# Stores of the first two batches' rows issued by SyncE in place of GpSimd, in a kernel of memory attention and two matrix products, with its written order searched anew

## Chip, cores and metric

The kernel runs on one core of one Trainium2 chip. The metric is the device time of one execution in microseconds; before the change the median of three runs is 727.82 us (727.61 to 728.73).

## The reference

All data is float32. For each of 8 batches and 8 heads, with 576 rows of 64 elements and 32 memory slots:

```python
a = softmax(phi, axis=rows)                # phi: 8 x 8 x 576 x 32
k_m = einsum('bhsm,bhsd->bhmd', a, k)      # 32 x 64 for each head
v_m = einsum('bhsm,bhsd->bhmd', a, v)
scores = q @ k_m.T / 8
attn_out = softmax(scores) @ v_m           # 8 x 8 x 576 x 64
x = attn_out.transpose(0, 2, 1, 3).reshape(4608, 512)
r = maximum(x @ w_in, 0)                   # w_in: 512 x 2048
out = (r * r) @ w_out                      # w_out: 2048 x 512, out: 4608 x 512
```

## The kernel before

**Work for one batch.** `memory(b)` loads phi, k and v and forms the sums over rows by TensorE (`products`, L545). k and v come in two parts of the rows, five chunks and then four, through one buffer, the tile KV: the first part KV_0 is two loads of 640 KB (128 partitions x 4 x 320), the second part KV_5 two loads of 512 KB (128 x 4 x 256), and both are issued by SyncE (SP) at L495. Since there is one buffer, KV_5 of a batch can be loaded only when the products on KV_0 have run. `scores(b)` loads q in four pieces (q_0_0, q_0_1, q_1_0, q_1_1), each by four DMAs on SP (L816); a piece waits until VectorE (DVE) has transposed the piece before it (L819). Then, for 16 slices of 128 of the 2048 columns, `mm1` computes x @ w_in in three terms and two halves of 288 rows (L894, six matmuls for each half), ScalarE (ACT) and DVE square the positive part, and `mm2` adds the slice to four accumulators of 128 rows each (for each accumulator L929 and L930 with the high piece of the squares, then L932 with the low piece). The 64 rows of a batch that are left over are done for two batches together (`mm2_left`, L955).

**Order of batches.** The first four slices of batch 0 run first, then all of batch 1, then the rest of batch 0, then batches 2 to 7. The sums of the first four slices of batch 0 wait in two tiles, `part`, until the rest is added to them. While batches 0 and 1 run, the weights are loaded and decoded (tiles raw and work); q, k, v and phi of batch 2 are loaded while the rest of batch 0 runs.

**Stores.** `evac` copies a finished accumulator to SBUF and records a store (L989). For batches 0 and 1 a store covers all 128 rows of an accumulator, as two rows of every partition group (`2x64x512`, 256 KB): four such stores from the tiles o_0 and o_1 of batch 1 and four from the `part` tiles of batch 0; the left-over rows of both batches (tile ol) are two stores of 128 KB. From batch 2 on a store is 64 KB (`32x512`). GpSimd (POOL) issues all of them, but for the last batch, whose stores alternate between SP and ACT.

**What sets the order.** Every instruction group is recorded by `Plan.op` with its engine or two engines that it may run on, its cost and its tiles. `Plan.order` walks through the table PLACES, 3526 numbers that name the recorded groups in the order in which they are written out (a negative one means the second of two engines). So the table fixes the order on each engine's queue; what one queue waits for from another is set by the tiles. The costs in `Plan.order` replay the table and decide one thing only: before a TensorE group that is expected to find TensorE idle, `fill` (L427) adds matmuls on zeros. There are 72 of these, all within the first 46 us of the span.

Of the kernel before, what the change touches and what calls it, by code (L numbers as in the profile page):

```python
# [341 lines left out]
def tile_attention_moe(  # L342
# [21 lines left out]
    B, H, S, D = q.shape  # L364
    M = phi.shape[3]
    DM, FF = w_in.shape
# [603 lines left out]
    def evac(a, home, o, cols, add=False):  # L970
        final = cols[-1] == (B - 1, NC - 1)
        if final:
            home = home[0]
# [5 lines left out]
        n = 1 if final or cols[0][0] >= 2 else len(cols) // len({x[0] for x in cols})  # L979
# [115 lines left out]
```

## Time and profile before

| | |
|---|---|
| median of 3 runs | 727.82 us (727.61 to 728.73) |
| profiled execution, its own time | 726.3 us |
| its span in the trace | 724.5 us |
| TensorE busy with matmuls | 711.0 us (98% of the span) |
| VectorE busy | 457.6 us (63%) |
| ScalarE busy | 344.6 us (48%) |
| GpSimd busy | 52.7 us (7%) |
| mean granted TensorE clock | 0.996 of full speed |

The span runs from the first to the last recorded instruction of the profiled execution; its own time is 1.8 us longer, for what lies around it. Of the span TensorE is idle for 13.5 us in all, so the table alone says that the other engines matter where they make TensorE wait, and a look by stretches of the span has to tell where that is.

### The profile page before, as it was taken

What the parts mean: (1) busy time and instruction counts of PE and PEld (TensorE: products, weight loads), DVE (VectorE), ACT (ScalarE), POOL (GpSimd) and SP (SyncE); (2) the same over time, 40 slices, a digit from 0 to 9 for tenths busy, and PEclk for the clock granted to TensorE, in tenths of its full rate; (3) what the DMA queues carried; (4) which work ended last, traced back from release to release, by engine and by line L of the source; (5) the groups of instructions that cost most, each with busy time, mean ns of one, the idle gap of its engine ahead of it and who ended that gap; (6) DMA issues with size and microseconds to landing.
All of it is one profiled execution on the core that took longest, in us unless ns stands there. A gap on an engine that the chain in (4) does not pass through costs nothing.

```text
span 724.5 us, 13808 instructions
## 1 busy us (share of the span) xinstructions
PE 711.0 (98%) x5487; PEld 574.2 (79%) x5490; DVE 457.6 (63%) x1082; ACT 344.6 (48%) x788; POOL 52.7 (7%) x108
## 2 busy tenths in 40 slices
PE   8899999989999999999999999999999999999997
PEld 4478888877788888888887887888878887888886
DVE  5999999823874579545873347745587355854430
ACT  3589998744442343533542434552343333534330
POOL 0000000010001000210001100050002100060000
PEclk9999999999999999999999999999999999999999
DMA  9933643555036131342203211242311301030002
GB/s 336 345 128 96 197 148 117 162 148 162 1 98 173 32 97 33 101 145 62 62 1 98 86 42 57 61 133 70 99 32 30 115 1 32 1 91 1 1 1 72
DMA packets 40608, 66.46 MB, mean 92 GB/s; under 512 B 8224, under 2 KB 24608, under 8 KB 40544
## 3 DMA queue, kind: packets, MB, share of 16 engines
q1 hardware_dynamic: 32928, 56.77, 25.6%
q0 software_dynamic: 7136, 8.16, 4.2%
q8 instruction: 43, 0.70, 0.4%
q10 hardware_dynamic: 480, 0.66, 0.3%
q14 instruction: 21, 0.17, 0.1%
HBM read 56.10 MB, written 9.44 MB: 90 GB/s over the span
## 4 chain that ended last, share of the span: by engine, by line
PE 89%; DMA 5%; DVE 4%; ACT 1%; issue 0%; SPq 0%; DVEq 0%; ACTq 0%
PE h L894 26%; PE acc L929 16%; PE acc L932 16%; PE acc L930 15%; PE accl L955 6%; PE vwpv L786 4%; DMA raw<-in_moe_w_in_dram 2%; DMA KV<-in_v_dram 2%; PE pkv_pa L545 1%; PE pscpa L826 1%; PE pkv_pv L545 1%; DMA KV<-in_k_dram 1%; DMA raw<-in_moe_w_out_dram 0%; DVE work L463 0%; PE idle L427 0%
## 5 line engine op out<-in xcount | busy, mean ns | idle before, releaser
L894 PE MATMUL h<-ath,vw 128*128 128x288 f32 x1024 | 210.6, 296 | 0.1
L929 PE MATMUL acc<-wo,gh 128*128 128x512 f32 x512 | 204.0, 398 | 0.0
L930 PE MATMUL acc<-wo,gh 128*128 128x512 f32 x512 | 201.5, 394 | 0.0
L894 PEld LDWEIGHTS h<-ath,vw 128*128 128x128 f32 x1024 | 170.4, 188 | 20.3 <-ACT r L898 3.3
L932 PE MATMUL acc<-wo,glo 128*128 128x512 f32 x512 | 181.8, 397 | 0.0
L898 ACT ACTIVATE r<-h 128x288 f32<-128x288 f32 x173 | 68.4, 408 | 151.7 <-PE h L894 124.9
L932 PEld LDWEIGHTS acc<-wo,glo 128*128 128x128 f32 x512 | 94.7, 188 | 28.6 <-issue 8.8
L929 PEld LDWEIGHTS acc<-wo,gh 128*128 128x128 f32 x512 | 96.2, 188 | 25.7 <-issue 9.1
L900 ACT ACTIVATE gh<-r 128x512 fp32r<-128x512 f32 x128 | 80.6, 629 | 75.2 <-PE acc L930 58.3
L904 DVE TENSOR_TENSOR glo<-r,gh 128x512 fp32r<-128x512 f32 x128 | 87.5, 683 | 45.4 <-ACT r L902 19.8
L930 PEld LDWEIGHTS acc<-wo,gh 128*128 128x128 f32 x512 | 96.3, 188 | 17.1
L894 PE MATMUL h<-atl,vw 128*128 128x288 f32 x512 | 109.5, 295 | 0.0
L894 PEld LDWEIGHTS h<-atl,vw 128*128 128x128 f32 x512 | 82.1, 188 | 0.0
L989 POOL DMA_DIRECT2D out_dram<-o x84 | 42.7, 514 | 486.9 <-ACT o L398 401.5
L899 DVE TENSOR_SCALAR r<-h 128x288 f32<-128x288 f32 x83 | 37.0, 454 | 61.6 <-PE h L894 60.5
L902 ACT ACTIVATE r<-r 128x576 f32<-128x576 f32 x100 | 68.2, 683 | 2.1
L955 PE MATMUL accl<-wo,gl 128*128 128x512 f32 x192 | 48.3, 395 | 0.0
L905 DVE TENSOR_TENSOR gl<-r,gl 128x64 fp32r<-128x64 f32 x128 | 27.4, 217 | 26.1 <-ACT r L902 25.6
L955 PEld LDWEIGHTS accl<-wo,gl 128*128 128x128 f32 x192 | 35.4, 188 | 8.4 <-issue 1.0
L901 ACT ACTIVATE gl<-r 128x64 fp32r<-128x64 f32 x128 | 31.4, 251 | 19.4 <-DVE r L899 18.5
L903 DVE TENSOR_TENSOR r<-r 128x576 f32<-128x576 f32 x28 | 21.1, 754 | 20.1 <-ACT gl L901 13.4
L398 ACT CAST vw<-vwpv 128x256 fp32r<-128x256 f32 x48 | 16.8, 376 | 24.8 <-PE vwpa L786 18.3
(140 smaller groups left out, 707.6 us busy)
## 6 DMA issues: line engine op xcount, KB each, us to landing
q<-in_q_dram SPq DMA_DIRECT2D x96, 136.0 KB, 2.8
raw<-in_moe_w_in_dram SPq DMA_DIRECT2D x16, 512.0 KB, 4.9
raw<-in_moe_w_out_dram SPq DMA_DIRECT2D x16, 512.0 KB, 4.3
out_dram<-o POOLq DMA_DIRECT2D x80, 64.0 KB, 2.1
phi<-in_phi_dram SPq DMA_DIRECT2D x8, 576.0 KB, 5.2
KV<-in_v_dram SPq DMA_DIRECT2D x6, 640.0 KB, 4.4
KV<-in_k_dram SPq DMA_DIRECT2D x6, 640.0 KB, 6.0
KV<-in_k_dram SPq DMA_DIRECT2D x6, 512.0 KB, 6.0
```

The lines of the kernel that those rows point to most:

```text
L894: nc.tensor.matmul(p()[:, 0:n], V()[:, l, hh, c0:c0 + P], x()[:, hh, cs], start=(i == 0), stop=(i == 5))
L898: op({"ACT": 295, **({} if b < 2 else {"DVE": tt(n)})}, lambda e, cs=cs, n=n, p=p: nc.scalar.activation(r()[:, cs], p()[:, 0:n], AF.Relu) ...
L899: else nc.vector.tensor_scalar(r()[:, cs], p()[:, 0:n], 0.0, None, ALU.max), [p], [(r, h)])
L900: op({"ACT": 535}, lambda e: nc.scalar.activation(gh(), r()[:, 0:SM], AF.Square), [r], [gh])
L901: op({"ACT": 160}, lambda e: nc.scalar.activation(G()[:, 0, lc], r()[:, SM:S], AF.Square), [r], [(G, (b % 2, 0))])
L902: op({"ACT": act(S), **({} if b < 2 else {"DVE": tt(S)})}, lambda e: nc.scalar.activation(r(), r(), AF.Square) if e == "ACT" else nc.vecto ...
L904: vec({"DVE": tt(SM)}, lambda e: nc.vector.tensor_sub(glo(), r()[:, 0:SM], gh().bitcast(F32)), [r, gh], [glo])
L929: nc.tensor.matmul(a(), gh()[:, c], t()[:, 0], start=f0, stop=False)
L930: nc.tensor.matmul(a(), gh()[:, c], t()[:, 1], start=False, stop=False)
L932: nc.tensor.matmul(a(), glo()[:, c], t()[:, 0], start=False, stop=f1)
L955: nc.tensor.matmul(a(), G()[:, l, :], t()[:, w], start=(ff == 0 and n == 0), stop=(ff == NFF - 1 and n == 2))
L989: d(rows, o()[32 * j:32 * (j + n), :])
```

## The change

One line of `evac` gives the stores of more than 64 KB to SP where POOL issued them, and the size that the planner's replay reckons with for any such store is raised (a factor of 75 in place of 48). The table PLACES is replaced by another.

```diff
 PLACES = (
...
-            dma(store, 48 * n * DM * 4, [home], [], eng=("SP", "ACT")[j // n % 2] if final or b == B - 1 else "POOL")
+            dma(store, 75 * n * DM * 4, [home], [], eng=("SP", "ACT")[j // n % 2] if final or b == B - 1 else "SP" if n > 1 else "POOL")
```

`n` is 4 for the accumulators of batches 0 and 1 and 2 for their left-over rows, so ten stores move from POOL to SP: four of o_0 and o_1, four of the part tiles, two of ol. The stores of batches 2 to 6 stay on POOL. The counts of TensorE's groups are the same (1536 matmuls of L894, 512 each of L929, L930 and L932, 192 of L955); of the fill matmuls there are 71 in place of 72.

SP's queue around the loads of k and v of batch 2 (KV_1826 and KV_1978 before, KV_1825 and KV_1980 after the change) stood like this before:

```order
L495 DMA KV_0_1826<-in_v_dram 128x4x320
L495 DMA KV_0_1826<-in_k_dram 128x4x320
L816 DMA q_0_0_1865<-in_q_dram 32x2x544 x4
L495 DMA KV_5_1978<-in_k_dram 128x4x256
L495 DMA KV_5_1978<-in_v_dram 128x4x256
L816 DMA q_0_1_2000<-in_q_dram 32x2x544 x4
L816 DMA q_1_0_2074<-in_q_dram 32x2x544 x4
L495 DMA phi_2126<-in_phi_dram 128x4x288
```

and stands like this now:

```order
L495 DMA KV_0_1825<-in_k_dram 128x4x320
L495 DMA KV_0_1825<-in_v_dram 128x4x320
L816 DMA q_0_0_1865<-in_q_dram 32x2x544 x4
L495 DMA KV_5_1980<-in_v_dram 128x4x256
L495 DMA KV_5_1980<-in_k_dram 128x4x256
L816 DMA q_0_1_2007<-in_q_dram 32x2x544 x4
L989 DMA out_dram<-o_0_1993 2x64x512
L816 DMA q_1_0_2110<-in_q_dram 32x2x544 x4
L989 DMA out_dram<-o_1_1926 2x64x512
```

The first two stores of batch 1 now stand behind both KV_5 loads and behind q_0_1, one ahead of q_1_0 and one behind it; phi of the next batch follows later.

On POOL the stores had stood one behind the other, with nothing but the accumulators to wait for:

```order
L989 DMA out_dram<-o_0_1898 2x64x512
L989 DMA out_dram<-o_1_1910 2x64x512
L989 DMA out_dram<-part_983 2x64x512
L989 DMA out_dram<-part_1010 2x64x512
L989 DMA out_dram<-ol_2847 64x512 x2
```

and its queue has now, behind the last instruction of the preparation, the 64-KB stores of batch 2 alone:

```order
L613 MEMSET kb_0_382 128x256
L989 DMA out_dram<-o_0_3642 32x512
L989 DMA out_dram<-o_1_3660 32x512 x3
```

Later on SP's queue, around KV_5 of batch 3 (KV_2699) and KV_0 of batch 4 (KV_2809), the rest of the moved stores stands now between loads:

```order
L989 DMA out_dram<-o_1_1926 2x64x512
L816 DMA q_0_1_2425<-in_q_dram 32x2x544 x4
L495 DMA KV_5_2699<-in_k_dram 128x4x256
L495 DMA KV_5_2699<-in_v_dram 128x4x256
L816 DMA q_1_0_2717<-in_q_dram 32x2x544 x4
L989 DMA out_dram<-part_999 2x64x512 x2
L989 DMA out_dram<-part_1009 2x64x512
L495 DMA KV_0_2809<-in_k_dram 128x4x320
L495 DMA KV_0_2809<-in_v_dram 128x4x320
L989 DMA out_dram<-part_1009 2x64x512
L989 DMA out_dram<-o_0_1993 2x64x512
L495 DMA phi_2888<-in_phi_dram 128x4x288
```

The last store of o_1 stands ahead of these two KV_5 loads with a q piece between; behind them four stores of part and the last of o_0 stand ahead of the next phi.

On TensorE the second products of batch 2 (L545 on KV_5) stood before the change behind this work on the rest of batch 0:

```order
L929 MATMUL acc_4_0_2030<-wo_1099,gh_2040 128x512
L930 MATMUL acc_4_0_2030<-wo_1099,gh_2040 128x512
L932 MATMUL acc_4_0_2030<-wo_1099,glo_2057 128x512
L545 MATMUL pkv_pa<-KV_5_1978,phi_1018 32x128
```

and now behind this:

```order
L929 MATMUL acc_4_0_2026<-wo_1136,gh_1983 128x512
L930 MATMUL acc_4_0_2026<-wo_1136,gh_1983 128x512
L932 MATMUL acc_4_2_2013<-wo_1136,glo_2005 128x512
L545 MATMUL pkv_pa<-KV_5_1980,phi_731 32x128
```

Between the first products (on KV_0) and the second (on KV_5) there were 5 halves of L894 with six matmuls each, 10 pairs of L929 and L930, and 8 matmuls of L932; now there are 4, 9 and 6. The order of the other groups changes all through the program, by a few places for the most part.

## Rows read from the trace of the kernel before

**Rows 1.** Page, part 1: busy time of TensorE, share of the span, instructions.

```profile
PE 711.0 (98%) x5487; PEld 574.2 (79%) x5490; DVE 457.6 (63%) x1082; ACT 344.6 (48%) x788; POOL 52.7 (7%) x108
```

**Rows 2.** Windows of TensorE: stretch, length, busy (count), granted clock, DMA share, GB/s.

```profile
0.00:50.00 50.00, 42.94 (x609) 1.00 0.76 276
50.00:160.00 110.00, 107.60 (x793) 1.00 0.49 151
160.00:700.00 540.00, 540.00 (x4015) 1.00 0.23 64
```

**Rows 3.** Waits of TensorE, its longest: us in total, times, longest.

```profile
PE pkv_pa L545 <- DMA KV<-in_v_dram: 2.3, 1, 2.3
PE pvt L591 <- DVE kx L676: 1.5, 2, 1.0
```

**Rows 4.** Timeline of TensorE around that wait: start, duration, in brackets idle time before.

```profile
156.22 0.39 PE L932 MATMUL acc<-wo,glo 128*128 128x512 f32 x1
158.92 0.27 PE L545 MATMUL pkv_pa<-KV,phi 64*32 64x128 f32 x1 [2.31 <-DMA KV<-in_v_dram]
```

**Rows 5.** Timeline of SP, its DMA issues from 146 us: start, time to issue.

```profile
146.05 0.38 SPq L495 DMA_DIRECT2D KV<-in_k_dram  x1
146.47 1.34 SPq L495 DMA_DIRECT2D KV<-in_v_dram  x1
147.99 15.92 SPq L816 DMA_DIRECT2D q<-in_q_dram  x8
```

**Rows 6.** Tile KV, window 145:148 (KV_5 of batch 2): issue to landing.

```profile
DMA to landing us min/median/max: 11.2/11.7/12.3
```

**Rows 7.** Windows over the second products, all engines: the clock is third from last.

```profile
159.00:160.00 1.00, 1.00 (x52) 1.00 (x59) 0.00 (x0) 0.00 (x0) 0.00 (x0) 0.61 0.37 111
160.00:161.00 1.00, 1.00 (x31) 0.62 (x14) 0.00 (x0) 0.00 (x0) 0.00 (x0) 0.50 0.08 23
161.00:162.00 1.00, 1.00 (x4) 0.89 (x5) 0.62 (x1) 0.00 (x0) 0.00 (x0) 0.50 0.06 17
162.00:163.00 1.00, 1.00 (x4) 0.41 (x3) 0.78 (x5) 0.37 (x1) 0.00 (x0) 0.69 0.00 0
```

**Rows 8.** Timeline of POOL, 138 to 170 us: the four stores of batch 1.

```profile
142.97 0.95 POOL L989 DMA_DIRECT2D out_dram<-o  x1 [116.82 <-ACT o L398]
144.83 0.82 POOL L989 DMA_DIRECT2D out_dram<-o  x1 [0.92 <-ACT o L398]
150.16 1.59 POOL L989 DMA_DIRECT2D out_dram<-o  x2 [4.51 <-ACT gl L901]
```

**Rows 9.** Tile KV, window 134:137 (KV_0 of batch 2).

```profile
DMA to landing us min/median/max: 4.3/5.3/6.2
```

**Rows 10.** Tile KV, window 383:386 (KV_5 of batch 5).

```profile
DMA to landing us min/median/max: 4.1/5.5/6.8
```

**Rows 11.** Tile KV, window 473:475 (KV_5 of batch 6, among 64-KB stores).

```profile
DMA to landing us min/median/max: 5.5/6.5/7.5
```

**Rows 12.** Tile KV, window 312:314 (beside one big store of part).

```profile
DMA to landing us min/median/max: 7.2/9.9/12.6
```

**Rows 13.** Windows with two big stores in flight alone (224:226), and one (the others).

```profile
224.00:226.00 2.00, 2.00 (x43) 1.51 (x44) 0.00 (x0) 0.41 (x1) 0.00 (x0) 1.00 0.25 102
321.00:323.00 2.00, 2.00 (x35) 0.90 (x36) 0.51 (x2) 1.18 (x4) 0.00 (x0) 1.00 0.13 51
```

**Rows 14.** Chain that ended last, 143 to 166 us: start, time to the next, group.

```profile
142.96 0.23 PE acc L932
143.19 0.24 PE acc L929
143.90 0.80 PE h L894 x6
```

**Rows 15.** Window of all engines in the preparation; DVE is the third busy time.

```profile
30.00:40.00 10.00, 8.54 (x63) 4.56 (x64) 10.00 (x21) 6.12 (x13) 0.00 (x0) 1.00 0.69 270
```

**Rows 16.** Page, part 6: loads of q, size of one, median from issue to landing.

```profile
q<-in_q_dram SPq DMA_DIRECT2D x96, 136.0 KB, 2.8
```

270 rows, old and new, of the table PLACES are left out of this document.

## Prediction

> **What bounds the kernel now.** I read the page first: TensorE is busy with matmuls for 711.0 of 724.5 us [rows 1], so no other engine is the bound, and what a new order can win is the 13.5 us in which TensorE stands idle, and time in which its clock is low. The windows say where the idle time lies: 7.06 us in the first 50 us, 2.4 us from 50 to 160, none from 160 to 700 [rows 2]; the rest is the start of the tail. The waits name what ended each: the largest single one, and the only one over 0.3 us behind the first 50 us, is 2.3 us of the products of L545 for a load of KV [rows 3]. The timeline puts it at 156.22 to 158.92, ahead of the second products of batch 2 [rows 4]. The next view is SP's queue: that load, KV_5, was issued at 146.05 and 146.47 [rows 5] and took 11.2 and 12.3 us to land [rows 6], so the later one was there at 158.8.
>
> The stall costs more than itself. In the windows behind it the granted clock is 0.61, 0.50, 0.50 and 0.69 in the four microseconds from 159 to 163, and TensorE is busy for all of them [rows 7]: it has gone from the upper of its two levels, 2.4 GHz, to 1.2 GHz, after 2.3 us of standing idle. Work done at those shares leaves (1 - 0.61) + 0.50 + 0.50 + (1 - 0.69) = 1.70 us to be made up. Stall and clock together are 2.31 + 1.70 = 4.0 us.
>
> **Why the load is late.** Four stores of 256 KB are issued by POOL at 142.97, 144.83, 150.16 and just behind it [rows 8], two before the loads and two while they are in flight. In other places the same kind of load takes far less: 6.2 us for the later of the pair at 135 [rows 9], 6.8 at 384 [rows 10], 7.5 at 474 amid 64-KB stores [rows 11]; but 12.6 us at 312, beside one big store [rows 12]. How such a store can hold up a load of only twice its size shows where it is alone in flight: the DMA engines are 0.13 busy, which is 2 of 16, and move 51 GB/s [rows 13], so 262,144 bytes keep two engines for about 5.1 us, and a load that is spread over all sixteen ends with the part that these two carry. With two such stores in flight the share is 0.25 at 102 GB/s, so POOL's two stores lay on different pairs.
>
> **Part by part.** *The stall.* On SP's queue no big store now stands ahead of KV_5 since the preparation; the first stands behind both loads and a q piece, and SP gives out its transfers in order. So I take KV_5 at the price of the quiet rows: the later load lands 6.2 us after its own issue, the issue is 0.42 us behind the first [rows 5, 9], so 6.6 us after the first issue; bounds 6.6 and 7.9 (7.5 + 0.4, [rows 11]). The cover shrinks also. Before, TensorE worked from the first issue, 146.05, to 156.22 + 0.23 = 156.45, that is 10.4 us. The new order takes out one half of L894 (0.80), one pair (0.24 + 0.23, L930 taken like L929) and two of L932 (2 x 0.23) [rows 14], 1.73 us together, so 8.7 us are left. The load then has 2.1 us to spare, 0.8 in the worst of its bounds: stall and low clock both go, -4.0 us.
>
> *The stores on SP.* Ten issues move to SP, some 0.4 us each like its other issues [rows 5], on a queue that mostly waits (eight issues of q stretch over 15.92 us [rows 5]); POOL is free of about 0.8 us each [rows 8]. Both cost TensorE nothing while SP isn't late. What stands behind the stores counts more. The first stands ahead of q_1_0 of batch 2. At the prices of [rows 14] the order has about 7.3 us of TensorE work from the earliest issue of that piece to its use, and the store is free to go some 4 us ahead of the piece. A quiet q load takes 2.8 us [rows 16]; if it has to wait for the whole store, it lands 5.1 + 2.8 = 7.9 us after the store's issue, 3.9 after its own, and over 3 us are left. Three part stores stand ahead of KV_0 of batch 4: 5.1 us if they lie on different pairs, 15.3 if on one, against over 70 us of TensorE work in the order before that tile is used; phi has over 40. Price nothing; if the cover of q_1_0 were gone, the loss would be up to 1 us.
>
> The Trainium skill says where stores on SP would lie (DMA: Bandwidth & Descriptors, "Why a DMA increments its semaphore by 16 and not by 1"): the slowest dimension of both patterns sets how many engines a transfer uses, and one issued from SP takes the lowest-numbered of them, where GpSimd's take turns. The trace agrees with the number of engines and with the turns, 2 of 16 for one and 4 for two [rows 13]; that SP's would all lie on one pair no run here shows. By that rule the larger figure, 15.3 us, holds for the part stores, and the sum stays as it is; by it B, below, is the likelier the more stores go out together.
>
> *Other loads by the same reasoning.* KV_5 of batch 3 gets 8.6 us of cover with no big store in flight, hidden. KV_5 of batch 4 had over 15 us of cover and now has about 8.7, and up to nine 64-KB stores of batch 2 stand on POOL in the same stretch. Its nearest row is that of 474 us, 7.9 us, so it fits by 0.8; the other end is 12.6 + 0.5 = 13.1 us [rows 12], a stall of 4.4 us. I take the nearer row, which has the same stores beside it, where that of 312 has a big one.
>
> *The preparation.* In the first 46 us DVE is busy for all of it, 10.00 of 10 us [rows 15], and TensorE waits for it, by 1.5 us for kx for example [rows 3]. The new table shifts three small groups from DVE to ACT, which has 3.9 us of 10 free there, and swaps a few neighbours. As the work of DVE ahead of kx is the same, I take zero, and 0.6 either way as the bound, less than half of what this wait has. The one fill matmul fewer is idle time filled. The tail is written as before.
>
> **Sum.** 726.3 - 4.0 = 722.3 for the profiled execution. The median of the three runs lies 1.5 us above it, so 727.8 - 4.0 = 723.8 us.
>
> **Rivals.**
> *A, some of it comes back.* Another load, KV_5 of batch 4 first of all, misses its shrunk cover. Its spare time is 0.8 us; if it lands 10.0 us after its issue, half way from 7.9 to 13.1 or a little less, TensorE stalls 1.3 us and pays up to the 1.7 us of clock again: 4.0 - 3.0 = 1.0 gained, 726.8; a smaller miss gives 724.5 to 726. For it: the new order cuts this cover nearly by half. Against: the row with the same company.
> *B, q behind the store.* The big store holds up q_1_0 of batch 2, DVE's transposition is late and with it the scores: up to 1 us, 724.8. Against it are the 3 us left.
> *C, slower.* It isn't the big stores that delay KV_5, but the loads around it (q_0_1 behind it, with SP's own issue taking 1.34 us [rows 5]). Then it lands again 12.7 us after its first issue, at a cover of 8.7: stall 4.0 in place of 2.3, 727.8 + 1.7 = 729.5. It decides from 8.7 us on, and loses from about 11.0 us on. Against it: four pairs elsewhere that are issued alike, the slow one beside a big store [rows 9 to 12].
> *D, no change.* The order replaces one stall by another of like size in the preparation or elsewhere, or the bytes contend on the same engines whoever issues them: 727.8. The Trainium skill says of the latter (DMA: Bandwidth & Descriptors, "Rules for kernel authors") that spreading transfers over issuers gains no bandwidth, since all share the same sixteen engines. No run here tests that, and by it only the place of the stores in time matters, which does change here: two of the four left before the loads and now none.
>
> **How the numbers follow.** The forecast has 0.66; A 0.15, B 0.05, C 0.07, D 0.07. The likeliest gives 723.8, with 0.6 for the preparation and the 1.1 us between the lowest and the highest of the runs before, 722.3 to 725.2. The range takes in B and most of A: 722.2 to 726.4; beyond it are C, D and the worst of A, less than 0.2. A measurement of this kernel can tell 0.2%, that is 1.5 us, from no change. Faster by more than that means under 726.3: the forecast, B and two thirds of A, 0.81, less 0.02 for a slower preparation, 0.79. Within it: D and the rest of A, 0.13. Slower: C and a little of A, 0.08.
>
> **What would show it.** In the profile of the changed kernel the products L545 of batch 2 should have no wait for KV over 0.3 us, KV_5 should land 6.4 to 8.0 us after its first issue, and the windows behind it should have a granted clock of 1.00; the windows from 50 to 160 should show TensorE idle for less than 0.3 us. Big stores on SP should take 0.3 to 0.5 us to issue and 5 us or more to land, later ones longer. If KV_5 of batch 2 lands late with no big store in flight, C is right and my reason wrong. If it lands in time and the time is still above 726, the loss must show as a new wait of TensorE: at KV_5 of batch 4 (A), at q or its transposition (B), or in the first 50 us (D).

## The result, and the profile after

The changed kernel takes 721.71 us in the median of five runs (721.06 to 722.52), the kernel before beside it 727.61 us (726.74 to 728.73). The ratio is 0.9919 with a 95% interval of 0.9904 to 0.9933: 5.9 us faster, by the interval 4.9 to 7.0. The forecast was 4.0 us faster, 723.8, with a range down to 722.2: the sign and the mechanism held, the size didn't. The two profiled executions alone would have made the forecast look exact: 726.3 and 722.52 us, spans of 724.5 and 720.8.

Windows of TensorE in the changed kernel, columns as in [rows 2]:

```profile
0.00:50.00 50.00, 42.48 (x607) 1.00 0.74 275
50.00:160.00 110.00, 109.53 (x819) 1.00 0.47 148
160.00:700.00 540.00, 539.41 (x3993) 1.00 0.22 65
```

From 50 to 160 us TensorE is idle for 0.5 us in place of 2.4; from 160 to 700 there are 0.6 us that weren't there. The waits of TensorE from 50 to 700 us are down to one line, and it isn't a load of KV:

```profile
PE acc L932 <- DVE glo L904: 1.1, 2, 0.6
```

The stall of [rows 3, 4] is gone. SP's queue at that place, with the first store of o behind the loads:

```profile
147.02 0.38 SPq L495 DMA_DIRECT2D KV<-in_v_dram  x1
147.45 0.51 SPq L495 DMA_DIRECT2D KV<-in_k_dram  x1
148.13 1.78 SPq L816 DMA_DIRECT2D q<-in_q_dram  x4
149.96 0.68 SPq L989 DMA_DIRECT2D out_dram<-o  x1
```

The tile KV in the window 146.9:148, the one landing that the trace has:

```profile
DMA to landing us min/median/max: 5.9/5.9/5.9
```

This is the load of k: issued at 147.45, there at 153.3, against 11.2 and 12.3 us in [rows 6]. The timeline of TensorE shows what is left of the cover, the last work ahead of the second products and the first of them:

```profile
155.47 0.39 PE L932 MATMUL acc<-wo,glo 128*128 128x512 f32 x1
155.79 0.29 PE L545 MATMUL pkv_pa<-KV,phi 64*32 64x128 f32 x1
```

No time in brackets stands behind the second: TensorE didn't wait. From 147.02 to 155.47 + 0.23 = 155.70 the cover is 8.7 us, as worked out, and the load was there 6.3 us after the first issue. The clock stays up in the same stretch, where [rows 7] had it down for four microseconds:

```profile
155.00:170.00 15.00, 15.00 (x164) 1.00 0.52 152
```

What came in its place is small: the two waits of that line. One, 0.47 us at 112 us, lies ahead of the first moved store (149.96) and stands in the run of the new table with POOL issuing too (0.4), so it doesn't come of the issuer. It alone takes the stretch from 50 to 160 us over the 0.3 us of idle time that the prediction named as its sign. The other, 0.58 us at 250 us, comes of the stores. The chain that ended last leads to it from a load of q:

```profile
240.66 8.06 DMA q<-in_q_dram
248.92 0.78 DVE qT L819
249.84 0.46 DVE r L899
250.35 0.69 DVE glo L904
251.08 0.73 PE acc L932 x2
```

A piece of q for batch 3 took 8.1 us where 2.8 is usual [rows 16]. SP's queue ahead of it shows why:

```profile
211.29 6.70 SPq L989 DMA_DIRECT2D out_dram<-part  x3
218.09 4.91 SPq L495 DMA_DIRECT2D KV<-in_k_dram  x1
223.06 2.48 SPq L495 DMA_DIRECT2D KV<-in_v_dram  x1
225.59 2.55 SPq L989 DMA_DIRECT2D out_dram<-part  x1
228.18 3.36 SPq L989 DMA_DIRECT2D out_dram<-o  x1
231.64 4.74 SPq L495 DMA_DIRECT2D phi<-in_phi_dram  x1
239.34 1.75 SPq L816 DMA_DIRECT2D q<-in_q_dram  x4
```

Five big stores are issued from 211 to 231 us, and the issues among and behind them take 2 to 5 us each, in place of 0.4. In the windows, engine SP, the DMA share and GB/s stand last:

```profile
230.00:233.00 3.00, 1.00 0.13 50
245.00:248.00 3.00, 1.00 0.14 44
```

0.13 of 16 engines are two: all the stores that SP issued lie one behind the other on one pair, and it works them off until 248, with the parts of the loads behind them. That SP's narrow transfers take the lowest-numbered engines is what the Trainium skill states (DMA: Bandwidth & Descriptors, "Why a DMA increments its semaphore by 16 and not by 1"); the trace agrees as far as it can show it, with one pair for them all.

### The profile page after: what moved, and what is told of

It is laid out like the page before. It is cut to its first block, busy times and chain, and to the rows that moved or that the text cites. A ratio compares the mean times of both kernels' runs of the same rounds, so it can differ in the third digit from the quotient of the medians.

```text
span 720.8 us, 13802 instructions
## 1 busy us (share of the span) xinstructions
PE 707.9 (98%) x5486; PEld 573.6 (80%) x5489; DVE 459.3 (64%) x1077; ACT 350.4 (49%) x793; POOL 45.0 (6%) x98
## 4 chain that ended last, share of the span: by engine, by line
PE 85%; DVE 6%; DMA 4%; ACT 2%; issue 2%; SPq 0%; DVEq 0%
PE h L894 26%; PE acc L932 15%; PE acc L929 15%; PE acc L930 15%; PE accl L955 6%; PE vwpv L786 4%; DMA raw<-in_moe_w_in_dram 3%; PE pkv_pa L545 1%; DMA q<-in_q_dram 1%; PE pscpa L826 1%; DVE work L466 1%; DMA KV<-in_k_dram 1%; PE pkv_pv L545 1%; DVE wi L472 1%; ACT work L464 1%
## 5 line engine op out<-in xcount | busy, mean ns | idle before, releaser
L894 PE MATMUL h<-ath,vw 128*128 128x288 f32 x1024 | 210.3, 295 | 0.0
L929 PE MATMUL acc<-wo,gh 128*128 128x512 f32 x512 | 203.7, 398 | 0.0
L930 PE MATMUL acc<-wo,gh 128*128 128x512 f32 x512 | 201.4, 393 | 0.0
L894 PEld LDWEIGHTS h<-ath,vw 128*128 128x128 f32 x1024 | 171.1, 188 | 17.9 <-ACT r L898 1.0
L932 PE MATMUL acc<-wo,glo 128*128 128x512 f32 x512 | 177.9, 397 | 1.1 <-DVE glo L904 1.1
L929 PEld LDWEIGHTS acc<-wo,gh 128*128 128x128 f32 x512 | 96.1, 188 | 29.8 <-issue 15.4
L932 PEld LDWEIGHTS acc<-wo,glo 128*128 128x128 f32 x512 | 94.2, 188 | 26.4 <-issue 8.2
L930 PEld LDWEIGHTS acc<-wo,gh 128*128 128x128 f32 x512 | 96.1, 188 | 16.9
L894 PE MATMUL h<-atl,vw 128*128 128x288 f32 x512 | 109.5, 295 | 0.0
L894 PEld LDWEIGHTS h<-atl,vw 128*128 128x128 f32 x512 | 82.2, 188 | 0.0
L989 POOL DMA_DIRECT2D out_dram<-o x80 | 39.4, 498 | 561.2 <-ACT o L398 483.6
L955 PE MATMUL accl<-wo,gl 128*128 128x512 f32 x192 | 47.7, 394 | 0.0
L955 PEld LDWEIGHTS accl<-wo,gl 128*128 128x128 f32 x192 | 35.5, 188 | 8.3 <-issue 0.8
L905 DVE TENSOR_TENSOR gl<-r,gl 128x64 fp32r<-128x64 f32 x128 | 27.3, 217 | 15.3 <-ACT r L902 14.7
L796 DVE TENSOR_TENSOR vw<-vwpa,vw 128x256 fp32r<-128x256 f32 x64 | 25.6, 417 | 2.8 <-ACT vw L398 2.3
```

What stands on the lines that cost most here:

```text
L894: nc.tensor.matmul(p()[:, 0:n], V()[:, l, hh, c0:c0 + P], x()[:, hh, cs], start=(i == 0), stop=(i == 5))
L929: nc.tensor.matmul(a(), gh()[:, c], t()[:, 0], start=f0, stop=False)
L930: nc.tensor.matmul(a(), gh()[:, c], t()[:, 1], start=False, stop=False)
L932: nc.tensor.matmul(a(), glo()[:, c], t()[:, 0], start=False, stop=f1)
L955: nc.tensor.matmul(a(), G()[:, l, :], t()[:, w], start=(ff == 0 and n == 0), stop=(ff == NFF - 1 and n == 2))
L989: d(rows, o()[32 * j:32 * (j + n), :])
```

## The experiments

Where two kernels are compared by their times, they ran on one chip beside runs of the kernel before.

**The kernel before, again.** No edit; three more profiles, one of them with times.

> The kernel before, once more, for the 1.9 us by which the medians differ by more than the two profiled executions do. Theory: the stall at the second products of batch 2 is not the same in every execution, and the profiled one of before had a short one; then the executions spread over 2 us or more, the longer ones have a lower mean clock than 0.996, and this profile may show a stall and low clock worth more than 4.0 us. Rival: the executions scatter for reasons that have nothing to do with the change; then stall and clock are again worth 4.0 us to within 0.3, whatever the time of the profiled execution, and the median lies anywhere from 726.3 to 728.7.

> A third profile of the kernel before, for the spread of its stall. Theory: the loss at the second products of batch 2 (stall and low clock) lies between 4.0 and 6 us and goes with the time of the execution, as 4.0 us with 726.3 us and about 5 with 727.3. Rival: the time varies and this loss does not.

> A fourth profile of the kernel before, as the third. Theory: loss at the second products of batch 2 between 4.0 and 6 us, larger where the time of the execution is larger. Rival: the time varies and this loss does not.

The first of the three took 727.16 us in the median of 12 runs (726.07 to 729.64), before beside it 726.9 (726.07 to 730.25). The profiled executions took 727.27, 728.18 and 727.91 us. TensorE in the window 155:170, first in the execution of the rows ahead of the prediction (726.3 us):

```profile
155.00:170.00 15.00, 12.69 (x140) 0.89 0.58 177
```

then in the first repeat (727.27 us):

```profile
155.00:170.00 15.00, 11.89 (x124) 0.89 0.60 185
```

in the second (728.18 us):

```profile
155.00:170.00 15.00, 12.03 (x116) 0.77 0.61 186
```

and in the third (727.91 us):

```profile
155.00:170.00 15.00, 12.02 (x116) 0.77 0.56 172
```

The idle time is 15 less the busy time: 2.3, 3.1, 3.0 and 3.0 us. The clock takes 15 x (1 - 0.89) = 1.7 us in the first two and 15 x (1 - 0.77) = 3.4 in the others. Together the same place loses 4.0, 4.8, 6.4 and 6.4 us (in the last two up to 0.4 is counted twice, since the clock was down before the products began). The loss is larger in the longer executions, though the two longest don't differ by it; so the theory holds in the main, and its upper end of 6 was a little low. The profile that I read held the smallest of the four. The times of the first repeat say the same of more executions: of its twelve, the four with a mean clock of 0.995 took 727.39 to 729.64 us, the eight with 0.997 or more 726.07 to 727.27. (The 1.9 us of the first expectation are the 5.9 measured less the 4.0 forecast; the two profiled executions differ by 3.8, which leaves 2.1.)

**The new table, POOL issuing.**

```diff
-dma(store, ..., eng=("SP", "ACT")[j // n % 2] if final or b == B - 1 else "SP" if n > 1 else "POOL")
+dma(store, ..., eng=("SP", "ACT")[j // n % 2] if final or b == B - 1 else "POOL")
```

> The changed kernel with its table, but the ten stores issued by POOL again. Theory: the place of the big stores ahead of KV_5 is what matters; on POOL they leave at about 143 to 151 us as before, KV_5 lands 11 to 12.7 us after its first issue against a cover of 8.7, so TensorE stalls 2.5 to 4 us and pays 1.7 us of clock: 4 to 6 us above the changed kernel, 726 to 728. Rival: the new order of the other engines brought the gain; then it stays at about 721.7.

727.82 us, ratio to before 1.0013 (1.0000 to 1.0025): the gain is gone, as the theory has it, but not at the place it named. POOL's queue:

```profile
150.28 2.55 POOL L989 DMA_DIRECT2D out_dram<-o  x3 [123.84 <-ACT r L898]
205.82 1.59 POOL L989 DMA_DIRECT2D out_dram<-part  x2 [52.99 <-DVE part L976]
214.39 1.59 POOL L989 DMA_DIRECT2D out_dram<-part  x2 [6.97 <-DVE part L976]
```

In the new table the store that comes first waits for a copy of o that ACT begins at 149.39 (the bracket names the instruction that ACT ended just after it), and the others queue behind it on POOL. So KV_5 of batch 2, issued at 147.13, was ahead of them and landed in 3.9 and 5.3 us with no stall. The stall appears one batch later. KV_5 of batch 3 is issued at 208.44, just behind two stores of part. The tile KV, window 208:210, who waited and the time to landing:

```profile
  PE pkv_pa L545: 4.4, 1
...
DMA to landing us min/median/max: 11.4/11.9/12.4
```

TensorE loses 4.4 us there and, by the clock of 0.77 in the window 214:229, 3.4 more. The changed kernel has no such wait, because SP issues these stores behind KV_5 (211.29 against 208.34).

**The old table, SP issuing.**

```diff
-dma(store, ..., eng=("SP", "ACT")[j // n % 2] if final or b == B - 1 else "POOL")
+dma(store, ..., eng=("SP", "ACT")[j // n % 2] if final or b == B - 1 else "SP" if n > 1 else "POOL")
```

> The kernel before with its table, but the ten stores issued by SP. By the table two of the four stores of batch 1 then stand on SP's queue ahead of KV_5 and two behind it and a q piece. Theory: the issuer alone does not help; the two ahead lie on one pair of engines, 2 x 5.1 us, and KV_5 ends behind them, at about 155 to 158 us: a stall of up to 2 us and clock, 725 to 728, no more than 2 us faster than before. Rival: the issuer alone brings the gain, 722 to 724.

728.4 us, 1.0013 (1.0003 to 1.0024), so no gain. SP's queue and, below, the waits of TensorE from 50 to 700 us:

```profile
143.02 2.38 SPq L989 DMA_DIRECT2D out_dram<-o  x2
146.39 1.10 SPq L495 DMA_DIRECT2D KV<-in_k_dram  x1
147.54 1.14 SPq L495 DMA_DIRECT2D KV<-in_v_dram  x1
```

```profile
PE pkv_pa L545 <- DMA KV<-in_v_dram: 2.5, 1, 2.5
PE pvt L584 <- ACT kx L555: 1.5, 1, 1.5
PE acc L932 <- DVE glo L904: 0.8, 1, 0.8
```

Two stores ahead of the load on the same queue hold it up as much as on another: the one landing in the trace is 11.6 us. The time came out 0.4 us above the span that I gave: the stall is 2.5 us where I gave up to 2, and two further waits followed it.

**The old table, POOL issuing, each big store as two of 64 rows.**

```diff
 rows = rows.rearrange("(p c) e -> c p e", c=RC)[c // 2:(c + n) // 2]
+for y in range(n // 2):
+    d(rows[y], o()[32 * j + 64 * y:32 * j + 64 * y + 64, :])
+return
```

> The kernel before, POOL issuing, but each 256-KB store split into two of 64 rows, so that the slowest dimension is 64 in place of 2. Theory: it is the narrow spread of the big stores (2 of 16 engines) that delays KV_5; spread over sixteen, the same bytes cost the load about 1 to 3 us, KV_5 lands 8 to 10 us after its first issue within its cover of 10.4, and stall and clock go: about 4 us under before, 722 to 724. Rival: the bytes contend wherever they lie; KV_5 is late by 1 us or more and the time stays within 2 us of before.

722.62 us, 0.9937 (0.9918 to 0.9955). Nothing is moved; only the slowest dimension of the stores is 64 in place of 2. KV_5 of batch 2 in the window 145.5:149, and TensorE in 155:170:

```profile
DMA to landing us min/median/max: 4.8/6.1/7.3
```

```profile
155.00:170.00 15.00, 15.00 (x165) 1.00 0.50 155
```

The stall is gone with stores ahead of the load and beside it. The later load is there 7.7 us after the first issue, a little under the 8 to 10 expected; against the 6.2 of a quiet pair [rows 9] the same bytes, spread wide, cost it about 1 us.

**The same, cut by columns.**

```diff
+for y in (0, DM // 2):
+    d(rows[:, :, y:y + DM // 2], o()[32 * j:32 * (j + n), y:y + DM // 2])
+return
```

> The kernel before, POOL issuing, with each big store split into two by columns, 2x64x256, where the run with split stores cut by rows, 64x512. The number and the bytes of the transfers are the same as there, only the slowest dimension stays 2. Theory: the spread over engines decides, so nothing is won: KV_5 of batch 2 again lands over 11 us after its first issue, and the time is that of before or above, 726.5 to 729. Rival: the size of one transfer decides; then the stall goes as with the split by rows, 722 to 723.5.

728.49 us, 1.0008 (0.9999 to 1.0017). As many transfers of as many bytes as in the run before, with the slowest dimension left at 2, and KV_5 of batch 2 is late again, by which TensorE waits 2.8 us:

```profile
DMA to landing us min/median/max: 11.3/12.0/12.8
```

So it is the spread that decides, and not the size of a transfer.

**The new table, SP issuing, stores as two of 64 rows.** The changed kernel with the edit that makes two stores of 64 rows.

> The changed kernel, SP issuing, but each 256-KB store split into two of 64 rows. In the trace of the changed kernel SP's issues behind the big stores take up to 4.9 us, and q_1_1 of batch 3 lands 8.1 us after its issue, for which DVE waits 1.9 us and TensorE 0.74 us at 250 us. Theory: that is the queue of big stores on one pair of engines; spread over sixteen it goes, so 0.7 us under the changed kernel run beside it (about 0.1%), no issue of SP behind a store over 2 us, and no wait of TensorE at 250 us. Rival: the wait comes from the order of the new table itself and stays.

721.63 us against 722.39 for the changed kernel beside it. SP's issues behind the stores are short again:

```profile
211.61 4.89 SPq L990 DMA_DIRECT2D out_dram<-part  x6
218.33 0.39 SPq L495 DMA_DIRECT2D KV<-in_k_dram  x1
```

q_1_1 of batch 3 finds no queue (its pieces land within 3.2 us) and the wait at 250 us is not in the trace. The 0.76 us agree with the theory but are smaller than the intervals of the two ratios; the trace carries this verdict.

**Matmuls on zeros in the stall of the old kernel.**

```diff
-fill(int(o.gap / (FILL if o.start > LEAD else 400)), o.outs)
+fill(10 if o.seq == 838 else int(o.gap / (FILL if o.start > LEAD else 400)), o.outs)
```

> The kernel before with ten matmuls on zeros, some 2.2 us, written ahead of the second products of batch 2, where TensorE stands idle. Theory: the low clock behind the stall comes of the idle time, so that work in its place keeps the clock at 1.00 and 1.5 to 2 us come back: 725 to 725.5 against 726.9. The stall itself stays, filled. Rival: the clock falls for another reason, or the fill costs what it saves, since the load may land later or earlier: within 0.5 us of before.

726.34 us, 0.9983 (0.9973 to 0.9993), 1.5 us under before by the medians. The fill in the timeline, and TensorE in 155:170:

```profile
157.33 2.13 PE L429 MATMUL acc<-zero 128*128 128x512 bf16 x9
```

```profile
155.00:170.00 15.00, 13.40 (x144) 1.00 0.61 190
```

The group with `o.seq == 838` is the one that begins the second products of batch 2. The load is as late as in the first repeat of before (12.0 and 13.1 us in both), the clock stays at 1.00, and the place loses 1.6 us idle and 2.1 of fill, 3.7 in place of 4.8. What the clock costs behind the stall is thus a loss of its own. The gain is the least that I had expected; the time itself lies above the span that I gave, since the kernel before beside it took 727.8 and not 726.9.

**The changed kernel, again.** No edit.

> The changed kernel once more, to have its times beside those of the other kernels and of before on one chip. Theory: the stall that the change removes differs from execution to execution, so the changed kernel spreads less than before, by about 1.5 us in place of 4, and lies 5 to 6 us under it. Rival: the 5.9 us of the first comparison were partly chance; then 4.0 to 4.5 under before, with as wide a spread.

722.39 us (721.25 to 722.92), 0.9926 (0.9908 to 0.9944), 5.4 us by the medians; before beside it spread from 726.17 to 729.70. Kernels without the stall spread by 0.8 to 1.7 us from their fastest to their slowest execution, over 5 or 6 of them; those in which TensorE stalls beside stores of POOL, unfilled, by 2.0 over 5 and by 2.7 to 4.2 over 12 to 29.

**The new table, POOL issuing, stores as two of 64 rows.** Both edits: the stores given back to POOL, and cut into two of 64 rows.

> The changed table with POOL issuing, each 256-KB store split into two of 64 rows. With the unsplit stores on POOL TensorE waited 4.4 us for KV_5 of batch 3 behind two part stores. Theory: with stores spread over sixteen engines it matters little who issues them and when: KV_5 of batch 3 lands 6 to 8.5 us after its first issue, hidden, and the time is within 1 us of the split stores on SP, 721 to 722. Rival: POOL's early issue takes bandwidth from KV_5 in any shape, and a stall of 1 us or more with low clock stays: 724 or more.

720.82 us (720.48 to 721.34), 0.9907 (0.9890 to 0.9924), the fastest of all, 1.6 us under the changed kernel beside it; the intervals of the two ratios overlap, but the executions hardly do (721.34 at most here, 721.25 at least there). From 50 to 700 us TensorE has no wait left:

```profile
50.00:160.00 110.00, 110.00 (x834) 1.00 0.50 154
160.00:700.00 540.00, 540.00 (x3991) 1.00 0.22 64
```

KV_5 of batch 3, behind the part stores on POOL as in the second experiment, lands in 4.1 and 5.8 us, the later one 6.2 us after the first issue. So with the spread stores POOL may issue ahead of the load, as the theory has it.

## Why the prediction was right in kind and short in size

*The bound, the place, the cause.* Right. The stall was worth going for, and it was the narrow spread of the big stores: the same stores on sixteen engines remove it, the same number of pieces on two don't. Rival C, that KV_5 is late by itself, falls with that, and so does D: the changed kernel's KV_5 had the cover of 8.7 us that I worked out and its load of k landed in 6.3 (the landing of v is not in the trace, but TensorE waited for neither). One reading was too simple: the slow pair at 312 us [rows 12], which I called issued like the others, stands 0.5 us behind a load of phi. With the split stores that pair, behind the same load, landed in 6.6 and 7.8 us in place of 7.2 and 12.6, which speaks for the store there too.

*The step that failed* is the size of the term: "Stall and clock together are 2.31 + 1.70 = 4.0 us." Both numbers were read rightly from the one profiled execution, and I carried them to the median, 1.5 us above it, as if that distance were a constant of the measurement. It was mostly this loss itself, which is another in each execution: 4.0, 4.8, and about 6 twice in four profiles, 5.2 on the mean. With the 0.7 us given back at 250 us that makes 4.5, and the two comparisons measured 5.9 and 5.4, with intervals that begin at 4.9 and 4.1. The spans of the profiled executions alone differ by 4.9 on the mean: 724.5, 725.5, 726.4 and 726.1 us before, 720.8 and 720.7 after. So the traces leave 0.4 us without a place; for the rest, the two profiled executions of the changed kernel took 0.8 and 0.1 us more than the medians of their runs. That the first two profiled executions differ by 3.8, so near the forecast, is luck: the one of before had the smallest loss of the four. What makes the loss differ is not shown. In all four the first store was issued 3.08 us ahead of the first load to within 0.01, and still the later load landed 12.3 us after its issue in one and 13.0 or 13.1 in the others. That the profile lay 1.5 us under the median of three runs was in the table ahead of the prediction, and the range took the 1.1 us between those three for the spread, where 29 executions of the same kernel spread by 4.2; the loss should have been given a range of its own.

*What protects the load.* I put it down to SP's queue. The runs divide it. At batch 2 the new table is enough, since POOL's first store waits for its copy until the load is under way; at batch 3 SP is needed, since there POOL would issue before the load. SP with the old table gains nothing. For stores on two engines, issuer and order only work as a pair.

*The stores on SP.* "Price nothing" was wrong by 0.58 us of waiting, 0.7 with the slower matmul behind it. I had reckoned 15.3 us for three part stores on one pair, but held it against KV_0 and phi alone; q_1_1 of batch 3, the next piece behind five stores and phi, was the one with little cover. I took the time of an issue as 0.4 us, and it was up to 4.9. So rival B happened, one batch later than I looked for it, and cost no more than it was given. The piece that I looked at, q_1_0 of batch 2, landed 3.9 us after its issue, as worked out, and nothing waited for it.

*KV_5 of batch 4.* The one landing in the trace, that of v, is 7.2 us after the first issue (297.66 to 304.89); the tile was used at 306.48, 1.6 us to spare: the nearer row was the right one, and A didn't happen.

*The preparation* has 0.5 us more idle time in the first 50 us, 7.5 for 7.1 in these two traces, inside its bound of 0.6. Four profiles of the kernel before lie between 6.8 and 8.6 us there, so this is no measured difference.

## What to carry to other kernels

Look at the slowest dimension of each store and not at its bytes: 256 KB as 2x64x512 delayed a load of the same stretch to 12 us, as two of 64x512 to 7. The Trainium skill says to put a dimension that is a multiple of 16 outermost (DMA: Bandwidth & Descriptors, "Rules for kernel authors"), and this case agrees: one edit of three lines in the old kernel won 4.3 us by the medians, most of the 5.4 to 5.9 that a new table for 3526 groups and the move to SP won together. On top of the new table the same lines won 1.6 more with POOL issuing, and with SP issuing 0.8, which is within the noise. And where a stall comes of a load that lands late among other transfers, one profile gives one draw of it: take several, or widen the range to what the spread of the times shows.

## What had not been expected of the hardware

An issue on SP is not a fixed cost: behind stores on two engines it took up to 4.9 us against 0.4, so that everything else on SP's queue is late too.

The low clock behind a stall doesn't last a fixed time. After 2.3 to 3.1 us of standing idle the loss was 1.7 us in two executions and 3.4 in two; after 4.4 us it was 3.4. With the old table on SP, TensorE stood idle for 2.5 us and then 1.5, and the clock stayed at its upper level:

```profile
155.00:170.00 15.00, 11.06 (x140) 1.00 0.53 158
```

What makes that difference these runs don't settle.
